# Mixing over tokens with z and the token weights as pairs of f16 numbers instead of pairs of f32r numbers

## The chip, the cores and the metric

The kernel runs on one core of a Trainium2 chip. Its engines are TensorE (PE; PEld is its weight load), VectorE (DVE), ScalarE (ACT), GpSimd (POOL) and SyncE (SP), which here issues the transfers. The metric is the device time of one execution in microseconds; where several runs are shown, their median.

## The reference

Attention with 8 heads over 8 batches of 576 positions, in a window of 128, and then on its output x (8 x 576 x 512) a layer that rotates x by learned angles, mixes over tokens and mixes over channels:

```python
scores = scale * np.matmul(q, k.transpose(0, 1, 3, 2))      # + a slope by head, window mask, softmax
x = attn_out.transpose(0, 2, 1, 3).reshape(B, S, H * D)     # 8 x 576 x 512
theta = x @ w_theta
zr, zi = x * np.cos(theta), x * np.sin(theta)
y = np.einsum('ts,bsd->btd', w_tok_r, zr) + np.einsum('ts,bsd->btd', w_tok_i, zi)
u = x + y
out = u + np.maximum(u @ w_ch, 0.0)
```

The weights come in as 64-bit floating point numbers (w_theta, w_tok_r, w_tok_i, w_ch) and are turned into 32-bit ones on the chip.

## The kernel before

An f32 product of full accuracy is put together from two parts of each factor: a high part (the number rounded to the f32r format) and a low part (what is left). Three matmuls, high by high, high by low and low by high, stand for one. For the mixing, the contraction runs over 1152 rows (576 tokens of zr and of zi), cut into nine blocks of 128. `wtk_hi` and `wtk_lo` hold the token weights of all nine blocks, `z_hi` and `z_lo` those of z of one batch. `mix` (L473) makes y in eight pieces of 128 channels by 288 tokens, each as 27 matmuls into one PSUM tile: 216 a batch, 1728 in all. z is the stationary operand, the weights move. VectorE then adds x from `xtf` (L478), ScalarE rounds u to `u_hi` and GpSimd makes `u_lo` for `channels` (L493), which holds 96 matmuls a batch.

In `turn`, per batch, x is transposed (L394), split and multiplied by w_theta (L414); VectorE and ScalarE reduce the angle and take cosine and sine; VectorE multiplies them by x (L438, L440), ScalarE rounds z to `z_hi` (L385) and GpSimd subtracts to `z_lo` (L386). The last of the nine blocks holds the 64 left-over tokens of both (L443, L444).

The program is staged. `start` runs attention for batch 0, and between its pieces a generator `unpack` turns the 64-bit weights into f32: per block of 128 rows two masks (L130, L132), an exponent on ScalarE (L134), two combinations (L139, L141) on VectorE, a product on GpSimd (L143), then the split into high on ScalarE (L149) and low on GpSimd (L150). Its four buffers are borrowed from tiles that are needed later (`u_hi`, `u_lo` and the two of `xtf`); a block's transfer can begin when its buffer's last user is done. w_theta comes first, the token weights next, w_ch last. From then on, for each b, `attend(b+1)` computes attention of the next batch with pieces of `mix(b)` put between, and then `turn(b+1)` alternates with `channels(b)`. The value products (`acc`, L341) already use pairs of f16 numbers for all but the first batch: `measure` takes the largest value of a head, `spread_scales` brings it to all partitions by a transposition (L213) and a small matmul (L220), and a power of two is made from its exponent bits (L222, L224).

The order on each engine is set by a scheduler that simulates the program once while it is built, with priorities given by `urgent`; each engine then runs its row strictly in that order.

## Time and profile before

| | us |
|---|---|
| median of 3 runs (lowest, highest) | 792.33 (790.96, 794.87) |
| the profiled execution | 790.2 |
| its span, first to last instruction | 788.4 |
| TensorE, VectorE, ScalarE, GpSimd busy | 733.9, 575.3, 481.9, 277.1 |
| chain that ended last | PE 65%, DVE 18%, ACT 10%, DMA 3%, issue 3% |
| of it the mixing matmuls, L473 | 23% |

A row of a group of instructions reads: line, engine, operation, written tile <- read tiles, shape, count | busy us, mean ns of one | idle time before and what ended it. A matmul's own time contains its way through the array, which overlaps with its neighbours; how dense matmuls follow each other is read from the starts of successive ones, or from the length of a stretch divided by their number. A row of the windows view has the stretch, its length, the busy time and count of PE, PEld, DVE, ACT and POOL, the mean granted TensorE clock, the share of the DMA engines and GB/s.

### The profile page before, as it was taken

The page shows a single profiled execution, that of the slowest core. Times are in us where ns is not written, and L with a number is a line of the kernel's source. Part 1 is how long each engine was busy: PE and PEld are TensorE (multiplying, and loading weights), DVE is VectorE, ACT ScalarE, POOL GpSimd, SP SyncE. Part 2 cuts the span into 40 slices and gives each one's busy share as a digit, 9 for nine tenths or more (in the row PEclk, how much of TensorE's full clock was granted, in tenths as well). Part 3 has the DMA queues.
Part 4 walks back from the last instruction along what each step waited for, and adds up shares of the span by engine and source line. Part 5 has one row for each costly group of instructions (what it writes and reads, how often), then busy time and mean ns, then how long its engine had stood idle before and what let it go on. Part 6 is the DMA issues. An engine that isn't in the chain of part 4 may idle for free.

```text
span 788.4 us, 16542 instructions
## 1 busy us (share of the span) xinstructions
PE 733.9 (93%) x6377; PEld 652.3 (83%) x6378; DVE 575.3 (73%) x1535; ACT 481.9 (61%) x962; POOL 277.1 (35%) x390
## 2 busy tenths in 40 slices
PE   6465799799999999999999999999999999999998
...
DVE  6999747778767877788777877797768877764711
...
PEclk9555579899999999999999999999999999999999
...
GB/s 270 151 150 132 40 74 22 31 66 65 81 28 54 73 65 54 24 65 82 65 40 65 66 54 54 47 64 80 54 24 65 65 71 53 1 2 31 31 1 61
DMA packets 29551, 49.66 MB, mean 63 GB/s; under 512 B 2592, under 2 KB 19104, under 8 KB 29472
## 3 DMA queue, kind: packets, MB, share of 16 engines
...
## 4 chain that ended last, share of the span: by engine, by line
PE 65%; DVE 18%; ACT 10%; issue 3%; DMA 3%; SPq 0%; DVEq 0%; ACTq 0%
PE mm L473 23%; PE mm L493 11%; PE mm L414 9%; PE s_ps L293 8%; PE t_ps L324 7%; PE acc L341 6%; ACT s_sb L304 3%; DVE f L429 2%; DVE s_sb L300 2%; PE mm L394 2%; DMA vb<-in_vx_dram 2%; ACT g L435 1%; DVE g L431 1%; ACT L304 1%; DVE xtf L139 1%
## 5 line engine op out<-in xcount | busy, mean ns | idle before, releaser
L473 PE MATMUL mm<-wtk_hi,z_hi 128*128 128x288 f32 x576 | 174.3, 307 | 1.0 <-ACT z_hi L385 0.7
L473 PE MATMUL mm<-wtk_lo,z_hi 128*128 128x288 f32 x576 | 167.9, 297 | 0.0
L473 PE MATMUL mm<-wtk_hi,z_lo 128*128 128x288 f32 x576 | 167.3, 301 | 0.2 <-POOL z_lo L386 0.2
L304 ACT ACTIVATE s_sb<-s_sb,fixed 128x256 f32<-128x256 f32 (+2 forms) x320 | 127.1, 466 | 56.0 <-DVE fixed L300 55.8
L300 DVE CUSTOM_DVE_ANT_0 s_sb<-s_ps,fixed 128x256 f32<-128x256 f32 (+2 forms) x320 | 105.2, 374 | 24.3 <-PE s_ps L293 9.9
L473 PEld LDWEIGHTS mm<-wtk_hi,z_hi 128*128 128x128 f32 x576 | 108.9, 190 | 4.9 <-ACT z_hi L385 0.9
L473 PEld LDWEIGHTS mm<-wtk_lo,z_hi 128*128 128x128 f32 x576 | 108.1, 189 | 0.4
L473 PEld LDWEIGHTS mm<-wtk_hi,z_lo 128*128 128x128 f32 x576 | 106.5, 189 | 2.1 <-POOL z_lo L386 0.4
L324 PE MATMUL t_ps<-fixed,s_sb 128*128 128x128 f32 x576 | 95.9, 297 | 12.2 <-ACT s_sb L304 11.8
L480 POOL TENSOR_TENSOR u_lo<-xtf,u_hi 128x288 fp32r<-128x288 f32 x64 | 52.4, 826 | 137.4 <-ACT u_hi L479 136.4
L386 POOL TENSOR_TENSOR z_lo<-g,z_hi 128x512 fp32r<-128x512 f32 x40 | 52.2, 1304 | 127.4 <-ACT z_hi L385 127.2
L324 PEld LDWEIGHTS t_ps<-fixed,s_sb 128*128 128x128 f32 x576 | 68.8, 150 | 21.6 <-ACT s_sb L304 17.9
L371 DVE SCALAR_TENSOR_TENSOR pt<-t_ps,pt 128x512 f16<-128x512 f32 x112 | 73.6, 681 | 11.3 <-ACT pt L370 11.0
L293 PE MATMUL s_ps<-kh,qh 64*128 64x256 f32 (+2 forms) x320 | 54.6, 337 | 15.1 <-DVE fixed L300 14.7
L237 POOL TENSOR_TENSOR kl<-kr,kh 128x576 fp32r<-128x576 f32 x32 | 46.0, 1438 | 63.8 <-ACT kh L236 63.3
L370 ACT ACTIVATE pt<-t_ps 128x512 f16<-128x512 f32 x112 | 61.5, 591 | 10.7 <-PE t_ps L324 10.4
L479 ACT CAST u_hi<-xtf 128x288 fp32r<-128x288 f32 x64 | 26.6, 428 | 62.5 <-DVE xtf L478 62.3
L341 PE MATMUL acc<-vh,pt 128*128 128x65 f16 x1008 | 60.1, 195 | 2.2 <-ACT pt L370 1.3
L341 PEld LDWEIGHTS <-pt 128*128 128x128 f16 x1512 | 52.3, 98 | 8.2 <-ACT pt L370 1.9
L293 PEld LDWEIGHTS s_ps<-kh,qh 64*128 64x128 f32 (+1 forms) x320 | 30.7, 188 | 33.5 <-DVE fixed L300 8.9
L429 DVE SCALAR_TENSOR_TENSOR f<-f,mm 128x512 f32<-128x512 f32 x32 | 22.0, 687 | 45.3 <-ACT f L428 45.3
L341 PE MATMUL acc<-vl,pt 128*128 128x64 f16 x504 | 54.9, 192 | 0.0
...
## 6 DMA issues: line engine op xcount, KB each, us to landing
...
xtf<-in_wtok_dram SPq DMA_DIRECT2D x4, 576.0 KB, 4.0
u_hi<-in_wtok_dram SPq DMA_DIRECT2D x3, 576.0 KB, 3.8
u_lo<-in_wtok_dram SPq DMA_DIRECT2D x2, 576.0 KB, 3.8
...
```

Source lines behind the costliest of these rows:

```text
L293: nc.tensor.matmul(ps[:qn, e, 256 * k:256 * k + kn], qm[rows, q0:q0 + qn], km[rows, k0:k0 + kn], start=(j == 0), stop=(j == len(self.terms ...
L300: nc.vector.tensor_tensor_reduce(out=sb, in0=ps[:qn, e, 256 * k:256 * k + kn], in1=bnd[:qn, c0:c0 + kn], scale=2.0 ** -((2 * self.p + e) % ...
L304: self.exp = nc.scalar.activation(sb, sb, AF.Exp, bias=least, scale=-1.0)
L324: nc.tensor.transpose(t_ps[:, off:off + 128], self.sc[i][:, 128 * j:128 * j + 128], ident)
L341: nc.tensor.matmul(av[:, i, :r.shape[-1]], l, r, start=(n == 0), stop=(n == len(prods) - 1))
L370: nc.scalar.activation(pt[:, 0], t_ps, AF.Copy, scale=2.0 ** PEXP)
L371: nc.vector.scalar_tensor_tensor(out=pt[:, 1], in0=t_ps, scalar=2.0 ** PEXP, in1=pt[:, 0], op0=ALU.mult, op1=ALU.subtract)
L386: nc.gpsimd.tensor_tensor(out=z_lo[:, c, :], in0=z, in1=z_hi[:, c, :].bitcast(F32), op=ALU.subtract)
L414: nc.tensor.matmul(t_ps, a[:, c * 128:c * 128 + 128], w[:, c, :], start=(k == 0 and c == 0), stop=(k == len(prods) - 1 and c == 3))
L473: nc.tensor.matmul(y_ps[:, :HALF], z[:, c, m * 128:m * 128 + 128], w[:, c, cs], start=(k == 0), stop=(k == 26))
L480: nc.gpsimd.tensor_tensor(out=u_lo[:, m, cs], in0=xtf[:, m, cs], in1=u_hi[:, m, cs].bitcast(F32), op=ALU.subtract)
L493: nc.tensor.matmul(o_ps[:, :HALF], w[:, c, e * 128:e * 128 + 128], u[:, c, cs], start=(k == 0), stop=(k == 11))
```

## The change

The four tiles of the mixing, `wtk_hi`, `wtk_lo`, `z_hi` and `z_lo`, become f16, and so do the 1728 matmuls on them. f16 has a small range of exponents, so both factors are scaled by powers of two:

- Each row s of the token weights is multiplied by a power of two taken from the sum of its absolute values (`sums`, `rows`). ScalarE makes the sum while it unpacks; three operations of one column on VectorE (`163`, and `power`) make the scale; ScalarE scales and rounds the high part, and VectorE, no longer GpSimd, makes the low part.
- Each row of z is multiplied by the inverse of that power (`invs`) times a power of two of the batch (`batch_scale`), which comes from the largest value of any head of this batch and the largest row sum. For the first batch the values' peaks are measured anew (`measure_first`, `scales_first`); later batches use the scales that the value products have already.
- z is scaled in the multiplication by x (one operation, as before). For the ninth block ScalarE scales while rounding, and VectorE makes the low part.
- When x is added to y, y is multiplied by the inverse power of the batch (`back`).

```diff
--- before.py
+++ after.py
...
@@ -35,7 +36,9 @@
 
 
 GROUP = 4
-RINGS = [("mx", 2 * NT, 4)] + [("den", NT, 6)] + [(name, GROUP, 3) for name in ("whole", "vs", "scale")]
+RINGS = ([("mx", 2 * NT, 4)] + [("den", NT, 6)] + [("whole", 1, 3), ("vs", GROUP, 3), ("scale", GROUP, 4)]
+         + [("whole0", 1, 1), ("vs0", 9, 1), ("scale0", 9, 1), ("sum", 9, 1),
+            ("row", 9, 1), ("inv", 9, 1), ("lim", 1, 1), ("t", 1, 2), ("zs", 9, 2), ("back", 1, 2)])
 MAGIC = 1.5 * 2.0 ** 23
 TURN = float(np.nextafter(np.float32(1.0 / (2.0 * np.pi)), np.float32(1.0)))
 RAD = float(np.nextafter(np.float32(2.0 * np.pi), np.float32(0.0)))
@@ -100,14 +103,27 @@
     wth_lo = const.tile([128, 4, DM], F32R, name="wth_lo")
     wch_hi = const.tile([128, 4, DM], F32R, name="wch_hi")
     wch_lo = const.tile([128, 4, DM], F32R, name="wch_lo")
-    wtk_hi = const.tile([128, 9, S], F32R, name="wtk_hi")
-    wtk_lo = const.tile([128, 9, S], F32R, name="wtk_lo")
+    wtk_hi = const.tile([128, 9, S], F16, name="wtk_hi")
+    wtk_lo = const.tile([128, 9, S], F16, name="wtk_lo")
+    sums, rows, invs, lim = (rings[name].take() for name in ("sum", "row", "inv", "lim"))
 
     nc.vector.memset(rebias, -float(916 << 23))
     for t in peaks:
         nc.gpsimd.memset(t, 0.0)
 
     ORDER = (0, 4, 1, 5, 2, 6, 3, 7, 8)
+
+    def power(out, of, top):
+
+        nc.vector.tensor_scalar(out=out.bitcast(I32), in0=of.bitcast(I32), scalar1=0x7F800000, scalar2=None,
+                                op0=ALU.bitwise_and)
+        nc.vector.tensor_scalar(out=out.bitcast(I32), in0=out.bitcast(I32), scalar1=-1.0,
+                                scalar2=float((2 * 127 + top) << 23), op0=ALU.mult, op1=ALU.add)
+
+    def inverse(out, of):
+
+        nc.vector.tensor_scalar(out=out.bitcast(I32), in0=of.bitcast(I32), scalar1=-1.0,
+                                scalar2=float((2 * 127) << 23), op0=ALU.mult, op1=ALU.add)
 
     def unpack(jobs, places):
 
@@ -141,11 +157,22 @@
             nc.vector.scalar_tensor_tensor(out=val, in0=raw[:, :, 0].bitcast(U32), scalar=2.0 ** -32, in1=ma,
                                            op0=ALU.mult, op1=ALU.add)
             nc.gpsimd.tensor_tensor(out=val, in0=val, in1=ex.bitcast(F32), op=ALU.mult)
+            if jobs[k][5] == "row":
+                c = jobs[k][3]
+                nc.scalar.activation(ex.bitcast(F32), val, AF.Abs, accum_out=sums[:, c:c + 1])
+                nc.vector.tensor_scalar(out=sums[:, c:c + 1], in0=sums[:, c:c + 1], scalar1=2.0 ** -100, scalar2=None,
+                                        op0=ALU.max)
+                power(rows[:, c:c + 1], sums[:, c:c + 1], WEXP)
 
         def split(k, t):
             _, hi, lo, c, w, scale = jobs[k]
             val = words(k, t)[2].bitcast(F32)
-            if scale is None:
+            if scale == "row":
+                s = rows[:, c:c + 1]
+                nc.scalar.activation(hi[:, c, :], val, AF.Copy, scale=s)
+                nc.vector.scalar_tensor_tensor(out=lo[:, c, :], in0=val, scalar=s, in1=hi[:, c, :],
+                                               op0=ALU.mult, op1=ALU.subtract)
+            elif scale is None:
                 nc.scalar.copy(hi[:, c, :], val)
                 nc.gpsimd.tensor_tensor(out=lo[:, c, :], in0=val, in1=hi[:, c, :].bitcast(F32), op=ALU.subtract)
             else:
@@ -169,7 +196,7 @@
                 tiles[k] = load(k)
 
     JOBS = ([(wth, wth_hi, wth_lo, c, DM, TURN) for c in range(4)]
-            + [(wtok, wtk_hi, wtk_lo, c, S, None) for c in ORDER])
+            + [(wtok, wtk_hi, wtk_lo, c, S, "row") for c in ORDER])
     LATE = [(wch, wch_hi, wch_lo, c, DM, None) for c in range(4)]
 
 
@@ -207,23 +234,55 @@
         nc.vector.tensor_scalar(out=most, in0=most, scalar1=2.0 ** -100, scalar2=None, op0=ALU.max)
         group_v[g] = vb, peak
 
+    def spread(peak, n, part):
+        m_ps = ps_m.tile([128, 512], F32, name="mm")
+        nc.tensor.transpose(m_ps[:, :128], peak, ident)
+        whole = rings["whole" + part].take()
+        nc.vector.tensor_reduce(out=whole, in_=m_ps[:, :128], axis=mybir.AxisListType.X, op=ALU.max)
+        diag = rings["vs" + part].take()
+        nc.vector.tensor_scalar(out=diag, in0=ident[:, :n], scalar1=whole, scalar2=None, op0=ALU.mult)
+        w_ps = ps_m.tile([128, 512], F32, name="mm")
+        nc.tensor.matmul(w_ps[:, :n], ones.broadcast_to([128, 128]), diag, start=True, stop=True)
+        scale = rings["scale" + part].take()
+        power(scale, w_ps[:, :n], VEXP)
+        return scale
+
+    z_scale = {}
+
+    def batch_scale(b, scales):
+
+        t, zs, back = (rings[name].take() for name in ("t", "zs", "back"))
+        nc.vector.tensor_reduce(out=t, in_=scales, axis=mybir.AxisListType.X, op=ALU.min)
+        nc.vector.tensor_scalar(out=t, in0=t, scalar1=lim, scalar2=whole_w[0], op0=ALU.min, op1=ALU.mult)
+        nc.vector.tensor_scalar(out=zs, in0=invs, scalar1=t, scalar2=None, op0=ALU.mult)
+        inverse(back, t)
+        z_scale[b] = zs, back
+
     def spread_scales(g):
         vb, peak = group_v[g]
-        m_ps = ps_m.tile([128, 512], F32, name="mm")
-        nc.tensor.transpose(m_ps[:, :128], peak, ident)
-        whole = rings["whole"].take()
-        nc.vector.tensor_reduce(out=whole[:, :1], in_=m_ps[:, :128], axis=mybir.AxisListType.X, op=ALU.max)
-        spread = rings["vs"].take()
-        nc.vector.tensor_scalar(out=spread, in0=ident[:, :GROUP], scalar1=whole[:, :1],
-                                scalar2=None, op0=ALU.mult)
-        w_ps = ps_m.tile([128, 512], F32, name="mm")
-        nc.tensor.matmul(w_ps[:, :GROUP], ones.broadcast_to([128, 128]), spread, start=True, stop=True)
-        scale = rings["scale"].take()
-        nc.vector.tensor_scalar(out=scale.bitcast(I32), in0=w_ps[:, :GROUP].bitcast(I32), scalar1=0x7F800000,
-                                scalar2=None, op0=ALU.bitwise_and)
-        nc.vector.tensor_scalar(out=scale.bitcast(I32), in0=scale.bitcast(I32), scalar1=-1.0,
-                                scalar2=float((2 * 127 + VEXP) << 23), op0=ALU.mult, op1=ALU.add)
+        scale = spread(peak, GROUP, "")
         group_v[g] = vb, scale
+        if g % 2:
+            c = rings["scale"].at + (g // 2 - 1) % 2 * 2 * GROUP
+            batch_scale(g // 2, fixed[:, c:c + 2 * GROUP])
+
+    whole_w = []
+
+    def measure_first(g):
+        nc.vector.tensor_reduce(out=peaks[0][:, GROUP * g:GROUP * g + GROUP], in_=group_v[g][:, :, :, :64],
+                                axis=mybir.AxisListType.XY, op=ALU.max, apply_absolute_value=True)
+
+    def scales_first():
+
+        peak = peaks[0]
+        nc.vector.tensor_reduce(out=peak[:, 8:9], in_=sums, axis=mybir.AxisListType.X, op=ALU.max)
+        nc.vector.tensor_scalar(out=peak[:, :8], in0=peak[:, :8], scalar1=2.0 ** -100, scalar2=None, op0=ALU.max)
+        scale = spread(peak, 9, "0")
+        whole_w.append(scale[:, 8:9])
+        inverse(invs, rows)
+        inverse(lim, scale[:, 8:9])
+        nc.vector.tensor_scalar(out=lim, in0=lim, scalar1=2.0 ** 120, scalar2=None, op0=ALU.mult)
+        batch_scale(0, scale[:, :8])
 
     def split_pair(p, raw):
 
@@ -377,13 +436,14 @@
     def turn(x_sb, st):
 
         xtf = uf.tile([128, 4, S], F32, name="xtf")
-        z_hi = big.tile([128, 9, DM], F32R, name="z_hi")
-        z_lo = big.tile([128, 9, DM], F32R, name="z_lo")
-        st.update(xtf=xtf, z_hi=z_hi, z_lo=z_lo)
+        z_hi = big.tile([128, 9, DM], F16, name="z_hi")
+        z_lo = big.tile([128, 9, DM], F16, name="z_lo")
+        zs, back = z_scale[st["b"]]
+        st.update(xtf=xtf, z_hi=z_hi, z_lo=z_lo, back=back)
 
         def split_z(c, z):
             nc.scalar.copy(z_hi[:, c, :], z)
-            nc.gpsimd.tensor_tensor(out=z_lo[:, c, :], in0=z, in1=z_hi[:, c, :].bitcast(F32), op=ALU.subtract)
+            nc.gpsimd.tensor_tensor(out=z_lo[:, c, :], in0=z, in1=z_hi[:, c, :], op=ALU.subtract)
 
         def columns(i):
 
@@ -435,14 +495,16 @@
                 nc.scalar.activation(g[:n], g[:n], AF.Sin, bias=halfpi[:n], scale=-RAD)
             st["sin"] = nc.scalar.activation(f[:n], f[:n], AF.Sin, scale=-RAD)
             if i > 0:
-                nc.vector.tensor_tensor(out=g, in0=x_sb[:, i, :], in1=g, op=ALU.mult)
-                split_z(i - 1, g)
-                nc.vector.tensor_tensor(out=f, in0=x_sb[:, i, :], in1=f, op=ALU.mult)
-                split_z(3 + i, f)
+                for c, z in ((i - 1, g), (3 + i, f)):
+                    nc.vector.scalar_tensor_tensor(out=z, in0=x_sb[:, i, :], scalar=zs[:, c:c + 1], in1=z,
+                                                   op0=ALU.mult, op1=ALU.mult)
+                    split_z(c, z)
             else:
                 nc.vector.tensor_tensor(out=g[:64], in0=x_sb[:64, i, :], in1=g[:64], op=ALU.mult)
                 nc.vector.tensor_tensor(out=g[64:], in0=x_sb[:64, i, :], in1=f[:64], op=ALU.mult)
-                split_z(8, g)
+                nc.scalar.activation(z_hi[:, 8, :], g, AF.Copy, scale=zs[:, 8:9])
+                nc.vector.scalar_tensor_tensor(out=z_lo[:, 8, :], in0=g, scalar=zs[:, 8:9], in1=z_hi[:, 8, :],
+                                               op0=ALU.mult, op1=ALU.subtract)
 
         order = (1, 2, 3, 4, 0)
         ahead = columns(order[0])
@@ -475,7 +537,8 @@
                         k += 1
                     if k < 27:
                         yield
-                nc.vector.tensor_tensor(out=xtf[:, m, cs], in0=y_ps[:, :HALF], in1=xtf[:, m, cs], op=ALU.add)
+                nc.vector.scalar_tensor_tensor(out=xtf[:, m, cs], in0=y_ps[:, :HALF], scalar=st["back"],
+                                               in1=xtf[:, m, cs], op0=ALU.mult, op1=ALU.add)
                 nc.scalar.copy(u_hi[:, m, cs], xtf[:, m, cs])
                 nc.gpsimd.tensor_tensor(out=u_lo[:, m, cs], in0=xtf[:, m, cs], in1=u_hi[:, m, cs].bitcast(F32),
                                         op=ALU.subtract)
@@ -587,6 +650,8 @@
             if new is not None:
                 for head in new.heads:
                     head.ready()
+            if new is not None and p % 2 == 0:
+                measure_first(p // 2)
             if p == 3:
                 load_values(2)
 
@@ -644,9 +709,10 @@
             pass
 
     first = []
-    st = [dict() for _ in range(B)]
+    st = [dict(b=b) for b in range(B)]
     x_sb = xp.tile([128, NT, DM], F32, name="x_sb")
     start(x_sb, unpack(JOBS + LATE, ((big, "u_hi"), (big, "u_lo"), (uf, "xtf"), (uf, "xtf"))))
+    scales_first()
     for p in range(H // 2, H // 2 + DEPTH):
         measure(p // 2)
         spread_scales(p // 2)
```

The order on the engines shows it at three places. The first is TensorE in a stretch of mixing in a middle batch (`mm` is the PSUM tile of y). Before:

```order
L473 MATMUL mm<-wtk_hi,z_hi 128x288
L473 MATMUL mm<-wtk_lo,z_hi 128x288
L473 MATMUL mm<-wtk_hi,z_lo 128x288
L324 MATMUL t_ps<-fixed,s_sb_8968 128x128 x4
L220 MATMUL mm<-fixed 128x4
L341 LDWEIGHTS pt
L341 MATMUL acc<-vh,pt 128x65
```

and now, in such a stretch:

```order
L535 LDWEIGHTS z_hi
L535 MATMUL mm<-wtk_hi,z_hi 128x288
L535 LDWEIGHTS z_hi
L535 MATMUL mm<-wtk_lo,z_hi 128x288
L535 LDWEIGHTS z_lo
L535 MATMUL mm<-wtk_hi,z_lo 128x288
```

The f16 matmul has its weight load as an instruction of its own in the row, as the value products have; z_hi is loaded for each of its two matmuls. The second place is VectorE while the token weights are unpacked, from the end of the first blocks to the first masks of a block that reuses the buffer `u_hi`. Before:

```order
L139 SCALAR_TENSOR_TENSOR xtf<-xtf 128x576
L130 TENSOR_SCALAR xtf<-xtf 128x576
L132 TENSOR_SCALAR xtf<-xtf 128x576
L141 SCALAR_TENSOR_TENSOR xtf<-xtf 128x576
L300 ISA s_sb_275,fixed<-s_ps,fixed 64x192
...
L300 ISA s_sb_276,fixed<-s_ps,fixed 128x256
L300 ISA fixed 128x1
L130 TENSOR_SCALAR u_hi<-u_hi 128x576
```

and now:

```order
L173 SCALAR_TENSOR_TENSOR wtk_lo<-u_hi,fixed,wtk_hi 128x576
L120 TENSOR_SCALAR fixed<-fixed 128x1
L163 TENSOR_SCALAR fixed<-fixed 128x1
L408 RECIPROCAL fixed<-fixed 128x5
...
L163 TENSOR_SCALAR fixed<-fixed 128x1
L118 TENSOR_SCALAR fixed<-fixed 128x1
L120 TENSOR_SCALAR fixed<-fixed 128x1
L173 SCALAR_TENSOR_TENSOR wtk_lo<-u_lo,fixed,wtk_hi 128x576
L146 TENSOR_SCALAR u_hi<-u_hi 128x576
```

The low part (L173) and the three small operations of each scale (L163, L118, L120) stand in VectorE's row; the last reader of the buffer `u_hi` is now there. The third place is GpSimd at the same time. Before:

```order
L143 TENSOR_TENSOR u_hi<-u_hi 128x576
L150 TENSOR_TENSOR wtk_lo<-u_hi,wtk_hi 128x576
L143 TENSOR_TENSOR u_lo<-u_lo 128x576
L143 TENSOR_TENSOR xtf<-xtf 128x576
L150 TENSOR_TENSOR wtk_lo<-u_lo,wtk_hi 128x576
L150 TENSOR_TENSOR wtk_lo<-xtf,wtk_hi 128x576
L143 TENSOR_TENSOR xtf<-xtf 128x576
```

and now:

```order
L159 TENSOR_TENSOR u_hi<-u_hi 128x576
L159 TENSOR_TENSOR u_lo<-u_lo 128x576
L159 TENSOR_TENSOR xtf<-xtf 128x576 x2
L345 MEMSET s_sb_441 64x64
L346 MEMSET s_sb_441 64x256
```

The nine subtractions of `wtk_lo` are gone from GpSimd; the products (L143, now L159) stay.

1 line of the change is left out of this document (added).

## Prediction

> **What bounds the kernel now.** I read the page first: engine totals and the three slice rows (40 slices of 19.7 us).
>
> ```profile
> PE 733.9 (93%) x6377; PEld 652.3 (83%) x6378; DVE 575.3 (73%) x1535; ACT 481.9 (61%) x962; POOL 277.1 (35%) x390
> PE   6465799799999999999999999999999999999998
> DVE  6999747778767877788777877797768877764711
> PEclk9555579899999999999999999999999999999999
> ```
>
> TensorE is full from about the eighth slice (157 us) on, at the full granted clock; in slices 1 to 3 it is half empty and VectorE is full. So there are two regimes, and the windows view puts numbers on them (columns: PE, PEld, DVE, ACT, POOL busy, then clock). The last two rows are the two halves of one steady batch: attention beside mixing, and the rotation beside the channel step.
>
> ```profile
> 20.00:88.00 68.00, 38.32 (x197) 32.18 (x198) 67.83 (x118) 36.41 (x68) 49.74 (x41) 0.53 0.41 128
> 88.00:156.00 68.00, 60.22 (x385) 49.25 (x384) 45.29 (x133) 43.97 (x88) 20.89 (x27) 0.80 0.15 45
> 499.00:547.00 48.00, 47.65 (x532) 43.97 (x532) 38.28 (x120) 34.87 (x78) 14.59 (x30) 1.00 0.22 65
> 547.00:585.00 38.00, 38.00 (x279) 33.20 (x278) 27.68 (x68) 23.21 (x41) 13.68 (x15) 1.00 0.16 49
> ```
>
> From 20 to 88 us VectorE works 67.83 of 68 us: unpacking the weights bounds the start. In a steady batch TensorE works 85.65 of 86 us, with VectorE at 66 and ScalarE at 58. There a nanosecond per matmul counts in full, and work added to the other engines is covered. Busy times overlap on TensorE, so what one matmul costs is its pitch, start to start. The chain of waits and the timeline give it:
>
> ```profile
> 742.52 10.51 PE mm L473 x79
> 556.17 2.76 PE mm L414 x12
> L505 PE MATMUL mm<-fixed x39: 379/379/631, 2.9 to 14.8; 128*128 128x512 bf16 x39
> 8.53 2.32 PE L505 MATMUL mm<-fixed 128*128 128x512 bf16 x10
> 159.38 0.20 PE L341 MATMUL acc<-vh,pt 128*128 128x65 f16 x1
> ...
> 160.19 0.19 PE L341 MATMUL acc<-vh,pt 128*128 128x65 f16 x1
> ```
>
> The f32r mixing matmul (288 columns) has a pitch of 10.51/79 = 133 ns; the f32r rotation (512 columns) 2.76/12 = 230 ns. The 16-bit filler, also 512 columns and also with a weight load before each, has ten matmuls in 2.32 us of which the last takes 379 ns: (2.32 - 0.38)/9 = 216 ns. The f16 value products (64 or 65 columns) run 27 from 159.38 to 160.19, 26 steps: 31 ns. Both 16-bit rows stand at full clock (the filler in slice 0, the values after the clock rose again). The 16-bit line through (65, 31) and (512, 216) and the f32r line through (288, 133) and (512, 230) are nearly parallel, 0.41 and 0.43 ns a column. So an f32r matmul costs a constant of 10 to 14 ns more, whatever its width.
>
> **The change, part by part.**
>
> *Mixing matmuls, the gain.* 1728 of them (three groups of 576) keep their shape and become f16. On the 16-bit line 288 columns cost 31 + 223 x 0.414 = 123 ns, against 133: 10 ns each, 17 us in all. Below, the f32r line's constant taken off at 512 columns (14 ns) gives 24 us; above, zero, if the constant belongs to something f16 keeps. I take 17, since both 16-bit rows reload weights before each matmul as the mixing does.
>
> The Trainium skill's page "TensorE: Matmul & The Clock Gate", section "Back-to-back issue gap", gives for sustained streams of weight load and matmul some 81 ns a matmul at 128 columns and 131 ns at 512. Between them 288 columns would cost about 102 ns (an estimate from that page), and the mixing would fall by 1728 x 31 = 54 us. The trace speaks against it: its 16-bit stream of 512 columns needs 216 ns, not 131. I keep it as a rival with a small chance.
>
> *Switches between kinds on TensorE.* The timeline shows what surrounds a mixing block:
>
> ```profile
> 528.02 0.29 PE L473 MATMUL mm<-wtk_hi,z_lo 128*128 128x288 f32 x1
> 528.15 0.20 PE L341 MATMUL acc<-vh,pt 128*128 128x65 f16 x1
> 528.19 0.20 PE L341 MATMUL acc<-vl,pt 128*128 128x64 f16 x1
> 528.22 0.38 PE L473 MATMUL mm<-wtk_hi,z_hi 128*128 128x288 f32 x1
> 528.44 0.29 PE L473 MATMUL mm<-wtk_lo,z_hi 128*128 128x288 f32 x1
> ```
>
> The first f32r matmul behind f16 is followed only after 220 ns instead of 133: some 87 ns lost when f32r starts behind short f16 matmuls. In the new order the mixing no longer loses this (14 places, 1.2 us), but f32r channel and rotation matmuls now follow f16 mixing at about 15 places and f32 transposes at some 55. Behind a 120 ns matmul there is more time to hide it, so I put it between -2 and +4 us, and take -1.
>
> *The start, the loss.* Here VectorE is the bound, so each operation on it counts. The lines and timeline of the start:
>
> ```profile
> L150 POOL TENSOR_TENSOR wtk_lo<-xtf,wtk_hi 128x576 fp32r<-128x576 f32 x4 | 7.0, 1766 | 0.0
> L150 POOL TENSOR_TENSOR wtk_lo<-u_hi,wtk_hi 128x576 fp32r<-128x576 f32 x3 | 5.4, 1812 | 1.5 <-ACT wtk_hi L149 1.5
> L150 POOL TENSOR_TENSOR wtk_lo<-u_lo,wtk_hi 128x576 fp32r<-128x576 f32 x2 | 3.5, 1772 | 0.0
> 50.27 1.93 POOL L150 TENSOR_TENSOR wtk_lo<-u_hi,wtk_hi 128x576 fp32r<-128x576 f32 x1
> 50.85 1.66 DVE L130 TENSOR_SCALAR xtf<-xtf 128x576 int32<-128x576 int32 x1
> 61.41 0.45 DVE L130 TENSOR_SCALAR u_hi<-u_hi 128x576 int32<-128x576 int32 x1
> 28.86 0.81 DVE L234 SCALAR_TENSOR_TENSOR ql<-qr,fixed,qh 128x576 fp32r<-128x576 f32 x1
> 29.59 0.75 DVE L141 SCALAR_TENSOR_TENSOR u_lo<-u_lo 128x576 f32<-128x576 uint32 x1
> 41.90 0.15 DVE L347 TENSOR_SCALAR fixed<-acc 128x5 f32<-128x5 f32 x1
> 41.97 0.74 DVE L141 SCALAR_TENSOR_TENSOR u_hi<-u_hi 128x576 f32<-128x576 uint32 x1
> 96.39 0.16 DVE L222 TENSOR_SCALAR fixed<-mm 128x4 int32<-128x4 int32 x1
> 96.59 0.17 DVE L224 TENSOR_SCALAR fixed<-fixed 128x4 int32<-128x4 int32 x1
> L205 DVE TENSOR_REDUCE peak<-vb 128x4 f32<-128x1280 f32 x14 | 20.7, 1482 | 10.8 <-DMA vb<-in_vx_dram 10.7
> u_hi<-in_wtok_dram SPq DMA_DIRECT2D x3, 576.0 KB, 3.8
> ```
>
> GpSimd loses its nine subtractions for wtk_lo (15.9 us). That is not idle gain: the same VectorE operation takes 0.45 us alone and 1.66 us beside such a subtraction, 1.2 us more. At 0 to 1.2 us each VectorE wins 0 to 10.8 us; not each one hits such an operation, so I take 0.9 each, 8 us.
>
> VectorE gains nine scaled subtractions of 576 columns, like L234 here (0.73 us to the next start, 1.2 us more when stretched in its turn): 6.6 to 17.4, I take 6.6, since the stretching goes by GpSimd operations, already counted. It gains 27 operations on one column (clamp, exponent mask, reversal); one that depends on the last, like L224 on L222, comes 0.2 us after it, and behind an independent one, like L347, the next starts after 0.07 us: 2 to 5.4, I take 3.5. And two reductions of the values of the first batch, 1.48 us each: 3.0. Together -8 + 6.6 + 3.5 + 3.0 = +5 us.
>
> A buffer of the unpacking ring now comes free behind the last VectorE subtraction, which stands in VectorE's row behind the small operations. The load that waits for it takes 3.8 us, and in the new order only some dozen short VectorE operations lie between u_hi's release and its next use, three rounds in all. 0 to +6, I take +2.
>
> ScalarE gains nine sums of absolute values of 576 columns. Nothing in the trace has that form; as long as a scaled copy, 0.8 us, they would make 7 us in a window where ScalarE has 31.6 us idle. I take nothing, and if they delay VectorE it is in the +2. The scales of the first batch (about 13 small VectorE operations, a transposition and a small matmul) come where VectorE has 22.7 of 68 us idle: nothing, or up to 2.6 us at 0.2 each without that cover. The start: **+7 us**, from +1 to +18 (the nine subtractions stretched in turn); all upper ends at once would be +34.
>
> *Steady batches.*
>
> ```profile
> L386 POOL TENSOR_TENSOR z_lo<-g,z_hi 128x512 fp32r<-128x512 f32 x40 | 52.2, 1304 | 127.4 <-ACT z_hi L385 127.2
> L438 DVE TENSOR_TENSOR g<-x_sb,g 128x512 f32<-128x512 f32 x32 | 23.5, 734 | 14.8 <-ACT g L435 14.4
> L429 DVE SCALAR_TENSOR_TENSOR f<-f,mm 128x512 f32<-128x512 f32 x32 | 22.0, 687 | 45.3 <-ACT f L428 45.3
> L478 DVE TENSOR_TENSOR xtf<-mm,xtf 128x288 f32<-128x288 f32 x64 | 27.4, 448 | 22.1 <-PE mm L473 22.1
> L496 DVE SCALAR_TENSOR_TENSOR xtf<-mm,xtf 128x288 f32<-128x288 f32 x64 | 28.6, 451 | 19.3 <-PE mm L493 18.6
> ```
>
> z times x with a scale (734 ns as two-tensor product, 687 as the scaled form) and x plus y (448 against 451) cost the same. One z_lo per batch moves from GpSimd (1.3 us) to VectorE (0.7 us), beside four small operations (0.8 us): 1.5 us on VectorE per batch. What hides it: VectorE's 20 idle us in 86. The wait on the scale of a batch is for a chain made a whole batch earlier, so nothing queues behind it. GpSimd's z_lo in f16 is in no row; 1.3 us as before, covered by its 58 idle us.
>
> *The sum* is made against the profiled execution, 790.2 us (span 788.4): 790.2 - 17 - 1 + 7 = 779.2. The median of the runs shown is 792.3, 2.1 above it. So the forecast is **781 us**.
>
> **The rivals.**
>
> *The start costs nothing.* If every subtraction taken from GpSimd frees its 1.2 us (-10.8 instead of -8), the small operations slip in between (2 us) and the ring never waits, the start is +1; with -2 for the switches: 774 us. For it: VectorE is stretched everywhere in the window. Against: its queue is in order, and each small operation waits for one on another engine.
>
> *The start eats it.* At +18 the time is 792, no change. It takes the nine new subtractions stretched in turn. Against: there are nine fewer GpSimd operations to stretch them.
>
> *VectorE becomes the bound beside the mixing.* TensorE's part of the 48 us shrinks by 216 x 10 ns to 45.8, while VectorE goes from 38.3 to about 39.8, 87%. If half the gain is lost to new waits: 790 us. Against: no wait of TensorE over 0.4 us is in that half now.
>
> *The constant stays.* If the extra 10 ns belong to a block where the weight changes with each matmul (the filler reloads the same tile), f16 mixing has 133 ns too. Only the start's cost is left: 781 + 17 = 798, slower. Against: the value products change their weights each time and run at 31 ns, in which no constant of 10 beyond the columns fits well. It decides as soon as the mean gain per matmul is under 4 ns, since 1728 x 4 ns = 7 us, the start.
>
> *The far shorter pitch.* At 102 ns instead of 123: 781 - 1728 x 21 ns = 745 us. The 216 ns of the filler speak against it.
>
> **How the numbers follow.** Forecast 0.60, own range 775 to 787 (the start from +1 to +13); the start costs nothing 0.12; the start eats it 0.11; VectorE the bound 0.07; constant stays 0.08; far shorter 0.02. A measurement of this kernel tells about 0.5% from no change, that is 788.4 to 796.3. Faster: 0.60 + 0.12 + 0.02 = 0.74; same: 0.11 + 0.07 = 0.18; slower 0.08. The range 770 to 792 takes in the forecast, the free start and the two without change; about 0.1 is left out for the constant and the far shorter pitch, and some at the edges.
>
> **What would show it.** The chain row of the last batch's mixing should give 123 ns a matmul, a steady batch 2.2 to 2.4 us less than 86. The window to 88 us should show VectorE still full with fewer stretched operations, and the first dense mixing about 7 us later. Wrong would be: a pitch of 133; a start longer by over 13 us; or new waits of TensorE on VectorE or ScalarE in the attention half.

## The result, and the profile after

The changed kernel takes 773.68 us (median of 4 runs, 773.66 to 773.72) against 793.6 us before (4 runs beside it, 790.96 to 796.35): ratio 0.975, 95% interval 0.971 to 0.979. That is faster, within the predicted range of 770 to 792 us, and 7 us below the forecast of 781 us. Ratios here and below leave disturbed runs out, so they are not always the quotient of the medians beside them.

The page of the changed kernel: engine totals, then the slices of TensorE, VectorE and the granted clock (40 slices, counted from 0).

```profile
PE 719.5 (93%) x6381; PEld 595.2 (77%) x6381; DVE 586.2 (76%) x1622; ACT 487.2 (63%) x980; POOL 248.8 (32%) x373
PE   7578799799999999999999999999999999999998
DVE  6998847978877988688777887798868887764722
PEclk9555558899999999999999999999999999999999
```

TensorE's busy time fell by 14 us and it is still the full engine; VectorE gained 11, GpSimd lost 28. The clock row is new in slices 5 and 6: half clock lasts longer than in the profile before.

Rows of the chain of waits of the changed kernel (start, length, engine, line, count). L535 is the mixing that was L473.

```profile
580.04 2.33 PE mm L535 x19
...
663.89 2.33 PE mm L535 x19
...
728.41 24.27 PE mm L535 x198
```

The last batch's mixing runs at 24.27/198 = 122.6 ns a matmul (before: 133). The first two rows are the same place in two neighbouring batches: 83.85 us apart, where a batch took 86.

The windows view, the same four stretches as in the prediction (the last two are moved with the batch):

```profile
20.00:88.00 68.00, 46.70 (x234) 38.50 (x235) 63.14 (x175) 45.89 (x94) 34.83 (x31) 0.50 0.41 129
88.00:156.00 68.00, 59.90 (x349) 47.29 (x349) 47.09 (x131) 40.59 (x79) 20.67 (x27) 0.70 0.15 44
487.00:533.50 46.50, 44.74 (x524) 37.26 (x523) 38.31 (x120) 33.40 (x74) 12.50 (x30) 1.00 0.20 58
533.50:571.50 38.00, 37.66 (x283) 31.92 (x282) 29.42 (x73) 24.23 (x44) 14.50 (x16) 1.00 0.19 61
```

Up to 88 us VectorE is no longer full (63.14 of 68), although it runs 175 operations instead of 118. In the steady batch TensorE now has holes: it is busy 82.40 of 84.5 us, where it was 85.65 of 86.

Where the 16.6 us between the two profiled spans (788.4 and 771.8) went is read from the first rotation matmul of each batch (L414 before, L474 after). The first rows of that line, before and then after, have the first start behind the durations:

```profile
L414 PE MATMUL mm<-wth_hi,x_hi x160: 387/394/537, 116.6 to 739.5; 128*128 128x512 f32 x160
```

```profile
L474 PE MATMUL mm<-wth_hi,x_hi x160: 387/393/792, 116.7 to 725.4; 128*128 128x512 f32 x160
```

| us | start to first rotation | first batch | next five batches, each | seventh | first rotation of the eighth to the end |
|---|---|---|---|---|---|
| before | 116.6 | 96.2 | 85.6 to 86.1 | 77.8 | 68.9 |
| after | 116.7 | 89.8 | 83.6 to 84.5 | 77.8 | 67.2 |

Nothing before the first rotation, 6.4 us in the first batch, 1.3 to 2.1 us in each of the next five. But this first batch is not the same work in both: its successor's first rotation comes behind 36 channel matmuls before and behind 25 after. A divide at the last mixing matmul of the first batch (198.6 and 196.5 us) leaves the same number of matmuls behind it. The windows view from there to the end, before and after:

```profile
198.60:788.40 589.80, 580.06 (x5266) 526.14 (x5264) 415.64 (x1136) 365.39 (x733) 184.12 (x277) 1.00 0.17 51
196.50:771.80 575.30, 560.31 (x5266) 471.54 (x5264) 428.59 (x1172) 364.92 (x734) 173.41 (x270) 1.00 0.17 52
```

So 2.1 us came ahead of this divide, which is what the first batch's 216 shorter matmuls give (216 x 10.4 ns = 2.2 us), and 14.5 us behind it: TensorE is busy 19.8 us less there and idle 5.3 us more.

### The profile page after: what moved, and what is told of

Same layout as the page of the kernel before. It is cut to its first block, busy times and chain, and to the rows that moved or that the text cites. A ratio compares the mean times of both kernels' runs of the same rounds, so it can differ in the third digit from the quotient of the medians.

```text
span 771.8 us, 16621 instructions
## 1 busy us (share of the span) xinstructions
PE 719.5 (93%) x6381; PEld 595.2 (77%) x6381; DVE 586.2 (76%) x1622; ACT 487.2 (63%) x980; POOL 248.8 (32%) x373
## 4 chain that ended last, share of the span: by engine, by line
PE 60%; DVE 20%; ACT 10%; DMA 6%; issue 3%; POOL 1%; SPq 0%; POOLq 0%; ACTq 0%; DVEq 0%
PE mm L535 19%; PE mm L556 11%; PE mm L474 9%; PE t_ps L383 7%; PE s_ps L352 6%; PE acc L400 6%; DMA vb<-in_vx_dram 3%; DVE s_sb L359 2%; DVE f L489 2%; PE mm L454 2%; ACT g L495 2%; DVE pt L430 1%; ACT s_sb L363 1%; ACT L363 1%; ACT L495 1%
## 5 line engine op out<-in xcount | busy, mean ns | idle before, releaser
L535 PE MATMUL mm<-wtk_hi,z_hi 128*128 128x288 f16 x576 | 163.0, 288 | 0.7 <-ACT z_hi L445 0.7
L535 PE MATMUL mm<-wtk_lo,z_hi 128*128 128x288 f16 x576 | 162.9, 288 | 0.0
L535 PE MATMUL mm<-wtk_hi,z_lo 128*128 128x288 f16 x576 | 159.4, 288 | 0.7 <-POOL z_lo L446 0.7
L535 PEld LDWEIGHTS <-z_hi 128*128 128x128 f16 x1152 | 110.6, 99 | 29.8 <-ACT z_hi L445 0.9
L383 PE MATMUL t_ps<-fixed,s_sb 128*128 128x128 f32 x576 | 102.9, 301 | 10.6 <-ACT s_sb L363 9.5
L383 PEld LDWEIGHTS t_ps<-fixed,s_sb 128*128 128x128 f32 x576 | 70.6, 153 | 21.6 <-ACT s_sb L363 15.3
L446 POOL TENSOR_TENSOR z_lo<-g,z_hi 128x512 f16<-128x512 f32 x32 | 42.9, 1341 | 100.2 <-ACT z_hi L445 100.1
L535 PEld LDWEIGHTS <-z_lo 128*128 128x128 f16 x576 | 56.2, 99 | 15.9 <-POOL z_lo L446 1.2
L400 PEld LDWEIGHTS <-pt 128*128 128x128 f16 x1512 | 57.1, 98 | 12.3 <-ACT pt L429 4.3
L352 PEld LDWEIGHTS s_ps<-kh,qh 64*128 64x128 f32 (+1 forms) x320 | 30.8, 189 | 27.6 <-DVE fixed L359 11.2
L556 PE MATMUL mm<-u_hi,wch_hi 128*128 128x288 f32 x256 | 49.8, 314 | 2.4 <-ACT xtf L467 1.0
L495 ACT ACTIVATE g<-g,fixed 128x512 f32<-128x512 f32 (+1 forms) x40 | 28.9, 723 | 36.4 <-DVE g L491 36.1
## 6 DMA issues: line engine op xcount, KB each, us to landing
xtf<-in_wtok_dram SPq DMA_DIRECT2D x4, 576.0 KB, 4.2
u_hi<-in_wtok_dram SPq DMA_DIRECT2D x3, 576.0 KB, 3.8
u_lo<-in_wtok_dram SPq DMA_DIRECT2D x2, 576.0 KB, 3.9
```

The source lines that it names most:

```text
L352: nc.tensor.matmul(ps[:qn, e, 256 * k:256 * k + kn], qm[rows, q0:q0 + qn], km[rows, k0:k0 + kn], start=(j == 0), stop=(j == len(self.terms ...
L383: nc.tensor.transpose(t_ps[:, off:off + 128], self.sc[i][:, 128 * j:128 * j + 128], ident)
L400: nc.tensor.matmul(av[:, i, :r.shape[-1]], l, r, start=(n == 0), stop=(n == len(prods) - 1))
L495: nc.scalar.activation(g[:n], g[:n], AF.Sin, bias=halfpi[:n], scale=-RAD)
L535: nc.tensor.matmul(y_ps[:, :HALF], z[:, c, m * 128:m * 128 + 128], w[:, c, cs], start=(k == 0), stop=(k == 26))
L556: nc.tensor.matmul(o_ps[:, :HALF], w[:, c, e * 128:e * 128 + 128], u[:, c, cs], start=(k == 0), stop=(k == 11))
```

## The experiments

All times are medians. "Half clock" is the time that TensorE spends at half its clock: the granted clock of a stretch is 0.50 or 1.00 (first and third row of the windows above), so it is 2 x (1 - mean clock) x span, taken for each run. "Unpacked" is the start of the last combination of the unpacking on VectorE (L141, L157). "To the divide" runs from the start to the last mixing matmul of the first batch, "behind it" from there to the end, with the same matmuls in every kernel. The columns from "unpacked" on are from the profiled execution.

| kernel | us (lowest to highest, runs) | ratio to before, interval | half clock, us | unpacked, us | first rotation, us | clock, 88 to 116 us | to the divide, us | behind it, us |
|---|---|---|---|---|---|---|---|---|
| before | 792.8 to 795.2 on three chips (783.6 to 799.2, 43) | 1 | 103 to 113 | 83.8 | 116.6 | 0.66 | 198.6 | 589.8 |
| after | 773.7 (773.7 to 773.7, 4) | 0.975 [0.971, 0.979] | 113 | 92.2 | 116.7 | 0.50 | 196.5 | 575.2 |
| f16_only | 766.1 (765.6 to 766.8, 4) | 0.966 [0.961, 0.970] | 93 | 84.1 | 112.3 | 0.78 | 188.9 | 574.5 |
| scale_f32r | 794.4 (791.1 to 797.3, 10) | 1.000 [0.998, 1.003] | 110 | 91.8 | 116.3 | 0.50 | 197.9 | 592.4 |
| low_on_dve | 780.9 (779.9 to 782.4, 4) | 0.984 [0.978, 0.989] | 86 | 80.7 | 111.5 | 0.73 | 189.5 | 591.2 |
| no_sums | 772.4 (766.0 to 776.7, 4) | 0.973 [0.966, 0.980] | 102 | 83.4 | 112.5 | 0.77 | 187.8 | 576.2 |
| after_vb3 | 773.6 (772.4 to 778.0, 4) | 0.981 [0.971, 0.991] | 97 | 92.5 | 115.3 | 0.67 | 196.4 | 575.6 |
| all_f16 | 761.3 (759.9 to 762.3, 4) | 0.964 [0.957, 0.971] | 109 | 92.5 | 116.9 | 0.50 | 194.8 | 565.5 |
| before_warm | 797.0 (795.8 to 806.6, 4) | 1.012 [1.001, 1.023] | 68 | 83.3 | 126.0 | 0.50 | 205.3 | 590.6 |
| after_warm | 771.9 (769.2 to 775.5, 4) | 0.978 [0.969, 0.986] | 60 | 91.7 | 117.2 | 0.59 | 197.3 | 574.5 |
| before_v4 | 784.8 (777.3 to 789.1, 12) | 0.992 [0.987, 0.997] | 97 | 85.3 | 114.8 | 0.50 | 192.9 | 589.5 |
| before_v5 | 792.5 (784.3 to 795.7, 12) | 1.001 [0.997, 1.006] | 111 | 83.4 | 120.5 | 0.50 | 201.4 | 591.4 |
| after_m10 | 771.1 (769.2 to 773.8, 6) | 0.976 [0.971, 0.981] | 96 | 91.9 | 117.0 | 0.50 | 196.9 | 574.9 |
| after_m9 | 775.3 (770.8 to 777.4, 6) | 0.981 [0.976, 0.986] | 113 | 90.3 | 113.8 | 0.68 | 195.1 | 576.0 |

### The two halves of the change apart

f16_only: the kernel before with f16 tiles, and nothing of the scaling.

```diff
-    wtk_hi = const.tile([128, 9, S], F32R, name="wtk_hi")
-    wtk_lo = const.tile([128, 9, S], F32R, name="wtk_lo")
+    wtk_hi = const.tile([128, 9, S], F16, name="wtk_hi")
+    wtk_lo = const.tile([128, 9, S], F16, name="wtk_lo")
...
-        z_hi = big.tile([128, 9, DM], F32R, name="z_hi")
-        z_lo = big.tile([128, 9, DM], F32R, name="z_lo")
+        z_hi = big.tile([128, 9, DM], F16, name="z_hi")
+        z_lo = big.tile([128, 9, DM], F16, name="z_lo")
```

> The kernel before with only the four mixing tiles in f16: no powers of two (so small low parts lose digits), the low part of the token weights still on GpSimd. Theory (the pitch does it): mixing matmuls 122 to 123 ns apart instead of 133, 1728 x 10 ns = 17 to 18 us less than before, of which new waits give back up to 5: 775 to 781 us, ratio 0.978 to 0.985; the rotation of the first batch starts at 116 to 118 us as before. Rival (much of the gain is GpSimd's relief at the start and in the first batch, not the pitch): the first batch's period stays near 96 us and the time is 783 us or more.

Measured: 766.1 us, 28.7 below before, more than the pitch can give: 18 us by the prediction's terms. Both expectations miss: the time lies below the theory's range, and the first rotation comes at 112.3 us and not at 116 to 118; the first batch's period is 87 us and not near 96. Of the 25.0 us between the two profiled spans 15.3 lie behind the divide (589.8 against 574.5) and 9.7 ahead of it.

scale_f32r: the changed kernel with f32r tiles, so all of the scaling and none of f16 (some rings of small tiles are shorter, to make room).

```diff
-    wtk_hi = const.tile([128, 9, S], F16, name="wtk_hi")
-    wtk_lo = const.tile([128, 9, S], F16, name="wtk_lo")
+    wtk_hi = const.tile([128, 9, S], F32R, name="wtk_hi")
+    wtk_lo = const.tile([128, 9, S], F32R, name="wtk_lo")
...
-        z_hi = big.tile([128, 9, DM], F16, name="z_hi")
-        z_lo = big.tile([128, 9, DM], F16, name="z_lo")
+        z_hi = big.tile([128, 9, DM], F32R, name="z_hi")
+        z_lo = big.tile([128, 9, DM], F32R, name="z_lo")
```

> The changed kernel with all its scaling and its VectorE subtractions, but the four mixing tiles in f32r again (four small rings cut by one or two places for room). Theory (scaling costs nothing here: the start is not longer and steady batches are covered): 789 to 796 us, ratio to before 0.995 to 1.005, mixing pitch 133 ns, first rotation at 115 to 119 us. Rival (the scaling costs the 7 us that the prediction gave it, and f16 brought more than 17): 798 to 802 us.

Measured: 794.4 us, as before to within 2 us. Its chain has the mixing at 26.44/198 = 133.5 ns:

```profile
744.70 26.44 PE mm L535 x198
```

The theory's time, pitch and first rotation all came. So the whole scaling, start and steady batches together, costs nothing in the medians on f32r, and f16 in place of f32r under the same scaling gives 794.4 - 773.7 = 20.7 us. But taken in the other order f16 gives 28.7 and the scaling costs 773.7 - 766.1 = 7.6. Something else differs by 8 us between these four kernels, and it lies in the start: behind the divide f16 is worth 15.3 us without the scaling and 17.2 us with it (592.4 - 575.2), and the scaling costs 2.6 us on f32r and 0.7 us on f16.

### The start: which of its operations counts

low_on_dve: the kernel before, with the nine subtractions for wtk_lo on VectorE.

```diff
-                nc.gpsimd.tensor_tensor(out=lo[:, c, :], in0=val, in1=hi[:, c, :].bitcast(F32), op=ALU.subtract)
+                eng = nc.vector if lo is wtk_lo else nc.gpsimd
+                eng.tensor_tensor(out=lo[:, c, :], in0=val, in1=hi[:, c, :].bitcast(F32), op=ALU.subtract)
```

> The kernel before with one edit: the nine low parts of the token weights are subtracted on VectorE instead of GpSimd. Theory (each GpSimd subtraction costs VectorE 0.9 us of stretching, about what its own subtraction costs): the first rotation starts within 2 us of before (114.6 to 118.6 us), time within 0.4% of before. Rival (VectorE is simply the bound there and pays 9 x 0.73 = 6.6 us): first rotation at 122 to 124 us, time 6 us longer.

Measured: 780.9 us, 14 less, outside what either had: one line of the start is worth nearly as much as the whole pitch. In its profile this lies ahead of the divide (189.5 against 198.6 us); behind it nothing is gained (591.2 against 589.8).

no_sums: the changed kernel without the nine sums and the 27 one-column operations, with fixed row scales.

```diff
+    nc.vector.memset(sums, 16.0)
+    nc.vector.memset(rows, 1024.0)
...
-            if jobs[k][5] == "row":
-                c = jobs[k][3]
-                nc.scalar.activation(ex.bitcast(F32), val, AF.Abs, accum_out=sums[:, c:c + 1])
...
-                power(rows[:, c:c + 1], sums[:, c:c + 1], WEXP)
```

> The changed kernel with fixed row scales: the nine sums on ScalarE and the 27 one-column operations on VectorE are left out. Theory (they slip in between at the start): within 1.5 us of the changed kernel, 772.2 to 775.2 us, first rotation at 115.5 to 117 us. Rival (each counts, as the prediction priced them, 3.5 us, and their order holds up the buffers, 2 us): 768 to 770 us, first rotation at 111 to 113 us.

Measured: 772.4 us, 1.3 below the changed kernel, with single runs over 10.7 us. In its profile, which is that of its fastest run (766.0 us), the unpacking ends 9 us earlier and the first rotation starts 4 us earlier; in the median that is not to be found.

### A third buffer for the values

In a steady batch of the changed kernel, 495 to 580 us, TensorE waits for this (waits view: instruction, releaser, us in all, times, longest):

```profile
PE s_ps L352 <- DVE fixed L359: 0.8, 1, 0.8
PE acc L400 <- DVE pt L430: 0.5, 1, 0.5
PE t_ps L383 <- ACT s_sb L363: 0.3, 1, 0.3
PE mm L556 <- ACT xtf L467: 0.2, 1, 0.2
PE acc L400 <- ACT pt L429: 0.2, 1, 0.2
```

Before, in the same place (499 to 585 us), it was one row:

```profile
PE t_ps L324 <- ACT s_sb L304: 0.3, 1, 0.3
```

Behind the longest stands, in the timeline of the changed kernel, `measure` on VectorE, which waits 1.82 us for a transfer of the values with the scores queued behind it:

```profile
525.86 1.49 DVE L232 TENSOR_REDUCE peak<-vb 128x4 f32<-128x1280 f32 x1 [1.82 <-DMA vb<-in_vx_dram]
```

after_vb3 gives the values a third buffer:

```diff
-    vbp = ctx.enter_context(tc.tile_pool(name="vbp", bufs=2))
+    vbp = ctx.enter_context(tc.tile_pool(name="vbp", bufs=3))
```

> The changed kernel with three buffers instead of two for the values (vbp), so that their transfer can start earlier. Theory (in steady batches VectorE stands in its row behind the peak measurement that waits for the values' transfer, and TensorE behind VectorE, some 1 us a batch that the shorter mixing laid open): 765 to 770 us, a steady batch 83.0 to 83.5 us instead of 83.6 to 84.5, no idle time of VectorE before the peak measurement. Rival (the rest of the missing gain is in the order, not in that wait): within 1.5 us of the changed kernel, 772 to 775.5 us.

Measured: 773.6 us, no gain, and the waits stand as they were (the first 0.9, the second 0.5); `measure` still waits 2.1 us for the transfer there. So the rival holds: a third buffer does not bring the transfer earlier. What does hold it stays open; another place for `measure` in VectorE's row was not tried.

### The constant of f32r at other widths

all_f16: the changed kernel with the rotation's and the channel step's tiles in f16 too, unscaled.

```diff
-    wth_hi = const.tile([128, 4, DM], F32R, name="wth_hi")
-    wth_lo = const.tile([128, 4, DM], F32R, name="wth_lo")
-    wch_hi = const.tile([128, 4, DM], F32R, name="wch_hi")
-    wch_lo = const.tile([128, 4, DM], F32R, name="wch_lo")
+    wth_hi = const.tile([128, 4, DM], F16, name="wth_hi")
+    wth_lo = const.tile([128, 4, DM], F16, name="wth_lo")
+    wch_hi = const.tile([128, 4, DM], F16, name="wch_hi")
+    wch_lo = const.tile([128, 4, DM], F16, name="wch_lo")
...
-            x_hi = xtp.tile([128, 512], F32R, name="x_hi")
+            x_hi = xtp.tile([128, 512], F16, name="x_hi")
...
-        u_hi = big.tile([128, 4, S], F32R, name="u_hi")
-        u_lo = big.tile([128, 4, S], F32R, name="u_lo")
+        u_hi = big.tile([128, 4, S], F16, name="u_hi")
+        u_lo = big.tile([128, 4, S], F16, name="u_lo")
```

> The changed kernel with the rotation's and the channel step's tiles in f16 too, without powers of two for them (digits are lost there; two unpacking buffers get tiles of their own, since u_hi and u_lo are smaller). Theory (every f32r matmul carries a constant of 10 to 14 ns, whatever its width and whatever moves): rotation pitch 216 ns instead of 230, channel pitch 122 to 123 instead of 133; 448 x 14 + 768 x 10 ns = 14 us, of which a third may go to new waits: 759 to 765 us. Rival (the steady batches now wait for the other engines, so a shorter pitch brings nothing more): 769 to 775 us with the same pitches.

Measured: 761.3 us, 12.4 below the changed kernel and within the theory's range. Its timeline has both shapes in a row, the channel step (L556, 288 columns) and the rotation (L474, 512 columns):

```profile
547.16 0.65 PE L556 MATMUL mm<-u_hi,wch_hi 128*128 128x288 f16 x4 [0.49 <-DVE f L489]
547.65 0.65 PE L556 MATMUL mm<-u_hi,wch_lo 128*128 128x288 f16 x4
548.14 0.65 PE L556 MATMUL mm<-u_lo,wch_hi 128*128 128x288 f16 x4
548.63 1.03 PE L474 MATMUL mm<-wth_hi,x_hi 128*128 128x512 f16 x4
549.49 1.03 PE L474 MATMUL mm<-wth_lo,x_hi 128*128 128x512 f16 x4
550.36 1.03 PE L474 MATMUL mm<-wth_hi,x_lo 128*128 128x512 f16 x4
551.22 0.60 PE L454 MATMUL mm<-fixed,x_sb 128*128 128x128 f32 x4
```

Twelve of 288 columns in 1.47 us, 122.5 ns each; twelve of 512 in 2.59 us, 216 ns. As f32r they took 133 and 230. So f32r costs 10 to 14 ns a matmul more than f16 at both widths. The Trainium skill's page "TensorE: Matmul & The Clock Gate", section "Wait — 56ns, not 53.3ns?", gives a matmul that follows another at full clock its columns at 2.4 GHz and some 2.5 ns: 122.5 ns at 288 columns and 215.8 at 512 (estimates from that page). The two stretches, 122.5 and 216 ns, agree with it to a nanosecond, as far as these rows tell, and not with the 131 ns at 512 of its section "Back-to-back issue gap".

### The clock in the start

In the start TensorE goes at half clock. before_warm and after_warm put eight filler matmuls behind each set of scores there, to bring the full clock earlier.

```diff
             def scores(tiles):
                 if new is not None:
                     new.scores(tiles)
                 pace(2 * len(tiles))
+                fill(8)
```

> The kernel before with eight more filler matmuls behind each piece of scores in the start (96 in all), to hold TensorE's clock up. Theory (before's runs lie between 789.7 and 796.8 us by how long the clock is halved in the start: mean clock 0.942 goes with 790, 0.926 with 796.5, 24 us of half clock for 6.5 us): mean clock 0.97 or more, 780 to 788 us, spread of the runs under 3 us. Rival (the start is bound by VectorE and the clock only goes along with it, or the fillers get in TensorE's way): 790 us or more.

> The changed kernel with the same 96 filler matmuls in the start. Theory (its clock was halved for 113 us at 0.927, so it has as much to gain as before): mean clock 0.97 or more, 762 to 768 us; the difference to before_warm is then the change without the clock, 17 to 21 us. Rival (fillers get in the way, or VectorE bounds the start at any clock): 772 us or more.

Measured: 797.0 and 771.9 us. Half clock fell from 113 to 68 and to 60 us, and the time did not follow, so as it was put the theory of the clock falls. The filler took away most of the half clock at 20 to 70 us, where VectorE is the bound, and left it between 88 and 116 us (0.50 and 0.59). The rival's other half, fillers in TensorE's way, is not excluded: the first rotation of before_warm starts at 126.0 us, 9 us later.

### The same operations in another order

All kernels above are ordered anew by the scheduler, and at the end of the first batch they fall into two orders. Behind the first piece of the rotation TensorE takes either 13 value products of the next batch's first heads before it goes on with the rotation, or only 3. (The expectations below call this value products ahead of transpositions; it is a mark by which the two are told, not a cause.) f16_only, low_on_dve and no_sums have the first, before, after, scale_f32r, after_vb3 and all_f16 the second (so have the two kernels with fillers, with 4 and 3). Two pairs were to take this apart: each pair moves one operation of the unpacking from GpSimd to VectorE, but for another block. before_v4 and before_v5 do get the one order and the other, 13 products and 3. after_m10 and after_m9 do not: their traces show 2 and 3 products there, so both have the second order, whatever the expectation of after_m10 says. before_v4 moves the low part of block 4 (before_v5 has 5 there):

```diff
-                nc.gpsimd.tensor_tensor(out=lo[:, c, :], in0=val, in1=hi[:, c, :].bitcast(F32), op=ALU.subtract)
+                eng = nc.vector if lo is wtk_lo and c == 4 else nc.gpsimd
+                eng.tensor_tensor(out=lo[:, c, :], in0=val, in1=hi[:, c, :].bitcast(F32), op=ALU.subtract)
```

after_m10 moves the product of job 10 (after_m9 has 9 there):

```diff
-            nc.gpsimd.tensor_tensor(out=val, in0=val, in1=ex.bitcast(F32), op=ALU.mult)
+            eng = nc.vector if k == 10 else nc.gpsimd
+            eng.tensor_tensor(out=val, in0=val, in1=ex.bitcast(F32), op=ALU.mult)
```

> The kernel before with one of the nine subtractions for wtk_lo (the second in order of unpacking, chunk 4) on VectorE instead of GpSimd, everything else as it was. Its twin before_v5 moves another one of the nine (the fourth, chunk 5). The two do the same operations on the same engines, but the scheduler, which works out its order from its own timeline, gives them different orders at the end of the first batch: here TensorE takes the remaining value products ahead of the transpositions of x, as in the three kernels whose first rotation began at 111.5 to 112.5 us (the f16 tiles alone, the low parts on VectorE, the scaling without its sums); in the twin the transpositions come first, as in before, after and the scaling in f32r, whose rotation began at 116.3 to 116.7. Theory (the order alone moves the start): first rotation at 111 to 113 us and 783 to 788 us, 5 to 10 us under the twin. Rival (what was gained there came from the operations removed or moved, in proportion): one subtraction of nine gives a ninth of the 14 us that all nine gave, 793 us, and the same as the twin within 1 us.

> The twin of before_v4: the kernel before with the fourth of the nine subtractions for wtk_lo (chunk 5) on VectorE, in the order with the transpositions of x ahead of the value products. Theory (order): first rotation at about 116.5 us and 792 to 796 us, as before. Rival (operations in proportion): 793 us, equal to before_v4 within 1 us.

> The changed kernel with one of the seventeen products of the unpacking (job 10) on VectorE instead of GpSimd. Its twin after_m9 moves the product of job 9. Same operations on the same engines in both, but this one has the order with the value products ahead of the transpositions of x. Theory (the order alone moves the start): first rotation at 111 to 113 us and 764 to 769 us, 5 to 9 us under the twin and under the changed kernel; against the f16 tiles alone, which have the same order (766.1), this is then the price of the scaling: 0 to 3 us. Rival (no effect of the order; the scaling costs its 7.6 us in any order): 773 to 775 us, equal to the twin.

> The twin of after_m10: the changed kernel with the product of job 9 on VectorE, in the order with the transpositions of x ahead of the value products. Both: as the changed kernel, 772 to 776 us, first rotation at about 116.7 us. If this one is fast too, neither holds, and one multiplication less on GpSimd was worth it by itself.

Measured: 784.8 against 792.5 us, and 771.1 against 775.3. The first pair is clear in the median, 7.7 us for one operation moved for the one block or the other, though single runs overlap; the proportional rival (equal within 1 us) falls. Its first rotations come at 114.8 and 120.5 us, nearly 6 us apart, but each later than the theory had. The second pair is no test of the order, since both have the same one; its runs overlap, and both lie near the changed kernel.

The table bears the order out. The four kernels with 13 products reach the divide at 187.8 to 192.9 us, the ten others at 194.8 to 205.3. Behind the divide the order does not show: with f32r mixing 589.5 to 592.4 us, with f16 mixing 574.5 to 576.2 (565.5 where all is f16). So what the change brings behind the divide, 13 to 18 us between any two of these kernels, is f16, and the other 8 us lie ahead of it and go with the order. Only the first pair changes the order with little else, and each kernel has one profile.

The length of the half clock goes with the time too. Over the 43 runs of the kernel before, one program, the time goes with it (86 to 123 us) at 0.35 us for each us, correlation 0.94. Put the kernels at 100 us by that slope: before 790.9, scale_f32r 790.9, f16_only 768.6, after 769.1, no_sums 771.7, after_m10 772.5, after_m9 770.8, after_vb3 774.6. The 8 us between the two ways round are gone there: f16 is worth 22 us either way, and the scaling costs 0 on f32r and 0 to 6 us on f16. The kernels with low parts moved are at 785.9 (before_v4), 785.8 (low_on_dve) and 788.6 (before_v5), so a few us of their gain remain beside the clock. But the slope is that of one program: within the ten runs of scale_f32r it is 0.19, within the six of after_m9 0.14, and the kernels with fillers lie far off the line (808 and 786 us at 100 us). This is a correlation; no run here set the clock alone, and order and half clock are not told apart.

Why the clock can count there, the windows view from 88 to 125 us shows, for before, after and f16_only:

```profile
88.00:125.00 37.00, 35.25 (x212) 29.17 (x211) 20.50 (x78) 19.67 (x42) 7.14 (x13) 0.69 0.23 67
```

```profile
88.00:125.00 37.00, 34.34 (x176) 29.05 (x175) 22.12 (x76) 16.58 (x34) 7.63 (x13) 0.56 0.22 65
```

```profile
88.00:125.00 37.00, 34.95 (x245) 29.70 (x245) 23.18 (x76) 22.91 (x47) 7.06 (x15) 0.83 0.16 51
```

TensorE is busy 93 to 95% of each, with VectorE at 55 to 63%, and gets 176, 212 or 245 matmuls done as the clock is 0.56, 0.69 or 0.83. This is a third regime between the two that the prediction saw: TensorE nearly full, at a clock that differs from kernel to kernel and, as the length of the half clock shows, from run to run.

## Why the prediction was right, and where not

**The mixing pitch, -17 us: right.** 133 ns became 122.6 (predicted 123), and all_f16 shows the constant at both widths. At 10.4 ns, 1728 matmuls give 18.0 us. The rivals of the constant that stays (798) and of the far shorter pitch (745) are out.

**Switches, -1 us: mis-sized, some -5 us, outside its bounds of -2 to +4.** The prediction counted the 14 places where mixing follows value products. The same loss stands behind the scores, where it did not look. Timeline, before and then after:

```profile
520.54 0.28 PE L293 MATMUL s_ps<-kl,qh 64*128 64x256 f32 x2
520.76 0.40 PE L473 MATMUL mm<-wtk_hi,z_hi 128*128 128x288 f32 x1
521.00 0.29 PE L473 MATMUL mm<-wtk_lo,z_hi 128*128 128x288 f32 x1
```

```profile
520.36 0.28 PE L352 MATMUL s_ps<-kl,qh 64*128 64x256 f32 x2
520.57 0.30 PE L535 MATMUL mm<-wtk_hi,z_lo 128*128 128x288 f16 x1
520.70 0.29 PE L535 MATMUL mm<-wtk_hi,z_hi 128*128 128x288 f16 x1
```

Behind the same scores the f32r matmul is followed after 240 ns, the f16 one after 130. Behind the divide, f32r matmuls of the mixing, the rotation and the channel step follow scores at 68 places before and at 31 after, and lose some 105 ns at each; they follow value products at 21 and at 2 places, 84 ns each. The f16 mixing loses 10 ns behind scores. Together this is about 5 us less. The loss feared for f32r behind f16 mixing did not come: at the 15 places the f16 matmul and the f32r one together take 256 ns, which is 123 + 133.

**The start, +7 us: this step failed, and its size is what the forecast missed.** On VectorE it was near the truth in sum: the last combination of the unpacking starts 8.4 us later. These are the rows of that line before (columns as for the rotation):

```profile
L141 DVE SCALAR_TENSOR_TENSOR xtf<-xtf x8: 678/728/1961, 16.3 to 77.1; 128x512 f32<-128x512 uint32 x4, 128x576 f32<-128x576 uint32 x4
L141 DVE SCALAR_TENSOR_TENSOR u_hi<-u_hi x5: 693/744/1844, 9.5 to 83.8; 128x576 f32<-128x576 uint32 x3, 128x512 f32<-128x512 uint32 x2
```

and after:

```profile
L157 DVE SCALAR_TENSOR_TENSOR xtf<-xtf x8: 675/712/746, 16.4 to 78.9; 128x512 f32<-128x512 uint32 x4, 128x576 f32<-128x576 uint32 x4
L157 DVE SCALAR_TENSOR_TENSOR u_hi<-u_hi x5: 682/745/751, 9.5 to 92.2; 128x576 f32<-128x576 uint32 x3, 128x512 f32<-128x512 uint32 x2
```

But the first rotation starts at 116.7 us, as before. The step took VectorE's delay as a delay of the dense work, one for one. Between lie 28 us in which TensorE is nearly full, and they don't wait for the end of the unpacking: over the table, unpacking that ends at 80.7 to 85.3 us goes with first rotations from 111.5 to 126, and at 90.3 to 92.5 with 113.8 to 117.2. scale_f32r, with the same start, is not slower at all. So the rival that the start costs nothing (774 us, 0.12) is what came, for another reason than it gave; that its 774 us is the measured time is luck, since its sum has 2 us for the switches, which brought 5, and none of the new waits below. Of the signs named for the start, VectorE full to 88 us and the first dense work 7 us later, both failed; that of fewer stretched operations held.

Term by term, on VectorE to 88 us:

```profile
L173 DVE SCALAR_TENSOR_TENSOR wtk_lo<-xtf,fixed,wtk_hi 128x576 f16<-128x576 f32 x4 | 4.4, 1096 | 0.0
L173 DVE SCALAR_TENSOR_TENSOR wtk_lo<-u_hi,fixed,wtk_hi 128x576 f16<-128x576 f32 x3 | 3.5, 1152 | 1.1 <-ACT wtk_hi L172 1.1
L173 DVE SCALAR_TENSOR_TENSOR wtk_lo<-u_lo,fixed,wtk_hi 128x576 f16<-128x576 f32 x2 | 1.6, 816 | 0.6 <-ACT wtk_hi L172 0.6
L146 DVE TENSOR_SCALAR u_hi<-u_hi 128x576 int32<-128x576 int32 x3 | 1.4, 456 | 2.1 <-DMA u_hi<-in_wtok_dram 2.1
L120 DVE TENSOR_SCALAR fixed<-fixed 128x1 int32<-128x1 int32 x9 | 1.2, 145 | 0.1
L118 DVE TENSOR_SCALAR fixed<-fixed 128x1 int32<-128x1 int32 x9 | 1.2, 140 | 0.0
L163 DVE TENSOR_SCALAR fixed<-fixed 128x1 f32<-128x1 f32 x9 | 1.2, 136 | 0.0
```

The nine sums on ScalarE were put at nothing; without them and the small operations (no_sums) the median is the same within its spread. The nine subtractions took 9.5 us (predicted 6.6; two of them were stretched to 1.83 and 1.96 us, the others last 0.81), the 27 small operations 3.6 (3.5), the two reductions of the first values 3.0 (3.0). The gain was mis-sized most: the 68 unpacking operations, grouped over the whole trace, fell from some 66 to 47 us, about 20 and not 8. In the rows above none of L157 is stretched any more (longest 751 ns, before 1961). That the unpacking still ended later is mostly waiting. Up to its last combination VectorE is busy 78.5 us (before 76.2), six more score operations among them, but idle 13.7 us (before 7.6). The waits view of VectorE from 20 us to there has no row before, and after these first:

```profile
DVE u_hi L146 <- DMA u_hi<-in_wch_dram: 2.7, 1, 2.7
DVE u_hi L146 <- DMA u_hi<-in_wtok_dram: 2.1, 2, 1.4
DVE wtk_lo L173 <- ACT wtk_hi L172: 1.7, 2, 1.1
```

So the buffer ring, put at 2 us, cost about 5 in waits for loads, more than half of it for w_ch, and ScalarE's high parts 1.7 more.

**Steady batches, covered, 2.2 to 2.4 us less each: right in kind, too high.** From first rotation to first rotation they gave 1.3 to 2.1 of 2.2 us, the seventh none. Behind the divide 14.5 us came, where 7 x 216 x 10.4 ns = 15.7 for the pitch and 5 for the switches make 20.7. New waits took most of the difference: by the waits view TensorE waited there for other engines 11.2 us in all, before 5.9. This is the sign that the prediction named for its rival "VectorE becomes the bound beside the mixing", new waits in the attention half; that rival has half the gain lost to them, and here they took a quarter.

**The sum.** Predicted -17 - 1 + 7 = -11. The two profiled executions are 16.6 us apart: -18 for the pitch, -5 for the switches, +5 for new waits, 0 for the start, and 1 to 2 us left over. The medians are 20 us apart; the other 3 us are that the profile before is of a run 3.4 us faster than the median of the four. So the forecast missed by the 7 us of the start. That the pitch alone then comes so near is luck in part: the switches and the new waits were both missed, and cancel.
